# Attention and gated MLP for one token: output rows 16 partitions apart for one store, a split last weight piece, and merged folds

## The chip, the cores and the metric

The kernel runs on one core of one Trainium2 chip. The metric is the device time of one execution in microseconds. "Faster" or "slower" needs 2%. There is one trace, of one execution, for each kernel.

## The reference

For four sequences of one token each, an attention block over the last 4096 cache positions and a gated MLP are mixed by a sigmoid gate:

```python
def reference(A_x, A_k_cache, A_v_cache, A_wq, A_wo, B_x, B_W_gate, B_W_up, B_W_down, gate_w):
    x = A_x                                               # [4, 1, 512]
    g = _sigmoid((x * gate_w).sum(-1, keepdims=True))
    a = _A_ref(x, A_k_cache, A_v_cache, A_wq, A_wo)       # 32 heads, 8 kv heads, window 4096, Dh 128
    b = _B_ref(x, B_W_gate, B_W_up, B_W_down)             # relu(gate) * up, then down; F = 1792
    return g * a + (1 - g) * b                            # [4, 1, 512] bf16
```

What matters for time: 81 MB are read once (sixteen 4 MB loads of K and V, the rest weights), and only 4 KB are written.

## The kernel before

SyncE issues all loads in order through four slots of 4 MB. The last load is `wo`, the 4 MB of output weights, cut into six pieces so that the matmuls of one piece run while the next lands. Eight sets (4 sequences x 2 groups of 4 kv heads) go through scores, softmax and `PV`. `OQ` ("fold") picks each head's own block out of the `PV` result and lays it out for the output matmul. `EOQ` scales it by 1/rowsum and by the gate into `oq`. `WO` accumulates in one PSUM bank on top of the MLP (`FFN`), the left half of the columns in rows 0 to 3, the right half in rows 64 to 67.

```python
WO_PIECES = ((0, 8), (8, 16), (16, 24), (24, 28), (28, 30), (30, 32))   # of 32 head rows per partition
OUTT = 2
OW = 512 // OUTT
OR = 128 // OUTT
# order of work at the end:  ... PV(6), PT(7), RS(1), GU, PV(7), FFN, OQ(1), WO(0..5)
# OQ(0), the fold of sets 0 to 3, runs in the middle of the kernel

def store(E, e, t):
    E.op(lambda: e.dma_start(out.rearrange("b o d -> (b o) d")[:, OW * t:OW * t + OW], osum[OR * t:OR * t + 4, :]),
         ev=("OUT", t), waits=[("OSUM",)], ctr=f"d_out{t}")          # t = 0 on SyncE, t = 1 on ScalarE

def OQ(g):                                        # 16 matmuls of 128 columns
    ...
        mm(banks[tr(key)][r:r + 64, 0:128], R["fold"][:, 2 * cc + t, c, :], osb[:, :, x:x + 32], ...)

def WO(p):                                        # two matmuls a head row: left and right half
    lo, hi = WO_PIECES[p]
    w = [("WO", p)] + [("E", "OQ", g) for g in range(2)]
    for i in range(lo, hi):
        for j in range(OUTT):
            mm(banks[ACC][OR * j:OR * j + 4, 0:OW], oq[:, i, :], Wo[:, i, OW * j:OW * j + OW], False, i == 31, ...)

def EOQ(g):                                       # VectorE; oq is [128, 32, 4]
    E.op(lambda: v.tensor_tensor(oq[r, :, :].rearrange("p i b -> p b i"), ...))

def FIN():                                        # VectorE: PSUM to SBUF, 128 x 256
    E.op(lambda: v.tensor_copy(osum[:, :], banks[ACC][:, 0:OW]), ev=("OSUM",), waits=[("WOP", len(WO_PIECES) - 1)])
```

(`...` marks cuts.)

Of the kernel before, what the change touches and what calls it, by code (L numbers as in the profile page):

```python
# [11 lines left out]
B = 4  # L12
# [9 lines left out]
NTR = 2  # L22
NSC = 3
BIG = 1.0e30
WO_PIECES = ((0, 8), (8, 16), (16, 24), (24, 28), (28, 30), (30, 32))
OUTT = 2
OW = 512 // OUTT
OR = 128 // OUTT

class _Plan:  # L30

# [70 lines left out]
def _alloc(nc, ctx):  # L102
    R = {}

    def sb(name, shape, dt):
        R[name] = ctx.enter_context(nc.sbuf_tensor(name, shape, dt))

    sb("slots", [128, NSLOT, 16384], BF16)
    sb("kt", [128, 4, 4096], BF16)
    sb("sc", [128, 2048], BF16)  # L110
    sb("pe", [128, 2048], BF16)
    sb("pT", [128, 2, 2048], BF16)
    sb("qblk", [128, NSET, 2, 144, 2], BF16)
    sb("xsb", [4, 512], BF16)
    sb("xT", [128, 16], BF16)
    sb("gwT", [128, 4], BF16)
    sb("osb", [128, 4, 512], BF16)
    sb("oq", [128, 32, 4], BF16)
    sb("identb", [128, 128], BF16)
    sb("identf", [128, 128], FP32)  # L120
    sb("ones", [128, 128], FP32)
    sb("ee", [16, 128], FP32)
    sb("e4", [16, 128], FP32)
    sb("rfold", [128, 128], FP32)
    sb("grpb", [128, 128], BF16)
    sb("own8", [128, 8], FP32)
    sb("scl", [128, 8], FP32)
    sb("maskl", [128, 128], BF16)
    sb("maskr", [128, 512], BF16)
    sb("maskf", [128, 512], BF16)  # L130
    sb("gwB", [128, 4, 128], BF16)
    sb("fold", [128, 4, 4, 64], BF16)
    sb("mx4", [128, 4], FP32)
    sb("rd32", [128, 8, 4], BF16)
    sb("negmax", [128, 2], FP32)
    sb("rowsum", [128, NSET], FP32)
    sb("recip", [128, 2, 4], FP32)
    sb("ge", [128, 2, 4], FP32)
    sb("gp", [128, 2, 4], FP32)
    sb("gg", [128, 2, 4], FP32)  # L140
    sb("hg", [128, 14, 4], BF16)
    sb("osum", [128, OW], BF16)
    R["psum"] = ctx.enter_context(nc.psum_tensor("bank", [128, 8, 512], FP32))
    return R


def _order():
    o = [("CONST", k) for k in ("mask", "grp", "rfold")] + [("XT",), ("Z",), ("Q",), ("QT",), ("KT", 0, 0), ("KT", 0, 1), ("SC", 0, 0)]
    o += [("KT", 0, 2), ("SC", 0, 1), ("KT", 0, 3), ("SC", 0, 2)]
    for s in range(1, NSET):  # L150
        o += [("KT", s, 0), ("SC", s - 1, 3)] + [("RS", 0), ("OQ", 0)] * (s == 5) + [("SW", s - 1)]
        o += [("KT", s, 1), ("PT", s - 1), ("SC", s, 0), ("KT", s, 2), ("SC", s, 1), ("KT", s, 3)]
        o += [("SC", s, 2)] + [("PV", s - 1)] * (s < NSET - 1)
    s = NSET - 1
    o += [("SC", s, 3), ("SW", s), ("PV", s - 1), ("PT", s), ("RS", 1), ("GU",), ("PV", s), ("FFN",), ("OQ", 1)]
    return o + [("WO", p) for p in range(len(WO_PIECES))]


# [28 lines left out]
def _program(nc, plan, R, aps):  # L187
# [17 lines left out]
    Wq = slot("wq").rearrange("p (t f) -> p t f", t=4)  # L205
    Wg, Wu = slot("wg")[:, 0:4 * FF], slot("wg")[:, 4 * FF:8 * FF]
    Wd = slot("wd")[:, 0:14 * 512]
    Wo = slot("wo", 0).rearrange("p (i c) -> p i c", i=32)
    grelu, hrow, hT = sc[:, 0:448], sc[:, 512:960], sc[:, 1024:1472]

    trf, scf = {}, {}
# [26 lines left out]
    def sc_free(key):  # L238
        n = scf[key] - NSC
        return [("E",) + sck[n]] if n >= 0 else [("INIT",)]  # L240

    def set_of(s):
        return s % 4, s // 4

    def ob(s):
        return banks[OB[s % 2]]

    def store(E, e, t):
        E.op(lambda: e.dma_start(out.rearrange("b o d -> (b o) d")[:, OW * t:OW * t + OW], osum[OR * t:OR * t + 4, :]),
             ev=("OUT", t), waits=[("OSUM",)], ctr=f"d_out{t}")  # L250

    def sync(e):
        E = _Eng(plan, e, "sp")
# [4 lines left out]
        for it in _dma_order():  # L258
# [4 lines left out]
            elif k == "gw":  # L263
                load(("GW",), "d_gw", gwT[:, :], gate_w.rearrange("(p t) -> p t", t=4))
            elif k == "wq":
                load(("WQ",), "d_wq", slot("wq"), A_wq.rearrange("(p t) f -> p (t f)", t=4), waits=w)
            elif k == "wg":
                load(("WG",), "d_wg", Wg, B_W_gate.rearrange("(p t) f -> p (t f)", t=4), waits=w)
            elif k == "wu":
                load(("WU",), "d_wu", Wu, B_W_up.rearrange("(p t) f -> p (t f)", t=4), waits=w)  # L270
            elif k == "wd":
                load(("WD",), "d_wd", Wd, B_W_down.rearrange("(p i) c -> p (i c)", i=14),
                     waits=w)
            elif k == "wo":
                lo, hi = WO_PIECES[it[1]]
                load(("WO", it[1]), f"d_wo{it[1]}", Wo[:, lo:hi, :], A_wo.rearrange("(p i) c -> p i c", i=32)[:, lo:hi, :],
                     waits=w)
            else:
                b, qq = set_of(it[1])
                src = (A_k_cache if k == "k" else A_v_cache)[b, 4 * qq:4 * qq + 4, SK - WIN:SK, :]  # L280
                load((k.upper(), it[1]), f"d_{k}{it[1] % 3}", slot(*it), src.rearrange("h (r c) d -> r h (c d)", r=32),
                     waits=w)
        for t in range(0, OUTT, 2):
            store(E, e, t)
        E.wait([("OUT", t) for t in range(OUTT)])

    def gpsimd(e):
        E = _Eng(plan, e, "pool")
# [19 lines left out]
        op(lambda: e.memset(R["scl"][:, :], -SCALE), ("SCL",))  # L308
        aff(R["own8"][:, :], R["scl"][:, :], [[-16, 8]], 0, ge_, 0.0, ("OWN", 0))
        aff(R["own8"][:, :], R["own8"][:, :], [[16, 8]], 15, ge_, 0.0, ("OWN", 1), mult=-1)  # L310
        op(lambda: e.memset(R["fold"][:, :, :, :], 0.0), ("FOLD0",))
        for g in range(8):
            v = R["fold"][:, g % 4, :, :]
# [2 lines left out]
    def tensor(t):  # L316
# [75 lines left out]
                    mm(ob(s)[r:r + 64, :], pT[:, s % 2, x:x + 64], vv[:, f, :, c:c + 2, :], (f, c) in ((0, 0), (0, 2)),  # L392
                       (f, c) in ((3, 12), (3, 14)), ev=("PV", s) if (f, c) == (3, 14) else None, waits=w, pos=(0, r))

        def OQ(g):
            key = ("OQ", g)
            r = 64 * g
            for t in range(2):
                for cc in range(2):
                    for c in range(4):  # L400
                        x = 256 * t + 128 * cc + 32 * c
                        first, lastmm = (t, cc, c) == (0, 0, 0), (t, cc, c) == (1, 1, 3)
                        mm(banks[tr(key)][r:r + 64, 0:128], R["fold"][:, 2 * cc + t, c, :], osb[:, :, x:x + 32], first,
                           lastmm, ev=key if lastmm else None, pos=(0, r),
                           waits=tr_free(key) + [("NORM", 4 * g + 3), ("FOLD", 7)] if first else ())

        def GU():
            for n, (W, key) in enumerate(((Wg, "WG"), (Wu, "WU"))):
# [8 lines left out]
        def FFN():  # L417
            for i in range(14):
                for j in range(OUTT):
                    x = 512 * i + OW * j  # L420
                    mm(banks[ACC][OR * j:OR * j + 4, 0:OW], R["hg"][:, i, :], Wd[:, x:x + OW], i == 0, False,
                       ev=("FFN",) if (i, j) == (13, OUTT - 1) else None, waits=[("E", "HT"), ("WD",), ("G",)],
                       pos=(0, OR * j))

        def WO(p):
            lo, hi = WO_PIECES[p]
            w = [("WO", p)] + [("E", "OQ", g) for g in range(2)]
            for i in range(lo, hi):
                for j in range(OUTT):
                    mm(banks[ACC][OR * j:OR * j + 4, 0:OW], oq[:, i, :], Wo[:, i, OW * j:OW * j + OW], False, i == 31,  # L430
                       ev=("WOP", p) if (i, j) == (hi - 1, OUTT - 1) else None, waits=w if (i, j) == (lo, 0) else (),
                       pos=(0, OR * j))

        fns = dict(CONST=CONST, XT=XT, Z=Z, Q=Q, QT=QT, SC=SC, PV=PV, SW=SW, RS=RS, OQ=OQ, WO=WO, GU=GU, FFN=FFN)
        for it in order:
# [4 lines left out]
    for it in order:  # L440
# [27 lines left out]
        elif k == "PV":  # L468
            act.append(("NORM", it[1]))
        elif k == "OQ":  # L470
            dve.append(("EOQ", it[1]))
    dve.append(("FIN",))

    def qd(n):
# [8 lines left out]
    def vector(v):  # L483
# [61 lines left out]

        def ERS(g):
            key = ("RS", g)
            E.op(lambda: v.reciprocal(recip[:, 0, :], banks[tr(key)][:, 0:4]), ev=("E",) + key, waits=[key])
            E.op(lambda: v.tensor_tensor(recip[:, 1, :], recip[:, 0, :], gg[:, 0, :], ALU.mult), ev=("RG", g),
                 waits=[("E",) + key, ("G",)])  # L550

        def EOQ(g):
            key = ("OQ", g)
            r = slice(64 * g, 64 * g + 64)
            E.op(lambda: v.tensor_tensor(oq[r, :, :].rearrange("p i b -> p b i"),  # L555
                                         banks[tr(key)][r, 0:128].rearrange("p (b i) -> p b i", b=4),
                                         bc(recip[r, 1, :].unsqueeze(2), 2, 32), ALU.mult), ev=("E",) + key,
                 waits=[key, ("RG", g)])

        def H():  # L560
            def by_i(t):
# [6 lines left out]

        def EHT():
            E.op(lambda: v.transpose(hT, hrow), ev=("HT",), waits=[("H",)])  # L570
            E.op(lambda: v.tensor_tensor(R["hg"][:, :, :], hT.rearrange("p (i b) -> p i b", b=32)[:, :, 0:4],
                                         bc(gg[:, 1, :].unsqueeze(1), 1, 14), ALU.mult), ev=("E", "HT"),
                 waits=[("HT",), ("G",)])

        def FIN():
            E.op(lambda: v.tensor_copy(osum[:, :], banks[ACC][:, 0:OW]), ev=("OSUM",), waits=[("WOP", len(WO_PIECES) - 1)])  # L576
# [6 lines left out]
    def scalar(a):  # L583
# [15 lines left out]
                 waits=[("GW",)])  # L599

        def NORM(s):
            E.op(lambda: a.activation(osb[:, s % 4, :], ob(s), ACTF.Copy), ev=("NORM", s),  # L602
                 waits=[("PV", s)] + ([("OQ", 0)] if s >= 4 else []))

        def GE():
            for u in range(2):
# [13 lines left out]
        fns = dict(ECONST=ECONST, GWB=GWB, EQ=EQ, GE=GE, RELU=RELU, EXP=EXP, NORM=NORM)  # L620
        for it in act:
            fns[it[0]](*it[1:])
        for t in range(1, OUTT, 2):
            store(E, a, t)

    return [("tensor", tensor), ("vector", vector), ("scalar", scalar), ("gpsimd", gpsimd), ("sync", sync)]

# [27 lines left out]
```

## Time and profile before

| | before |
|---|---|
| median of the first 3 executions | 197.54 us (197.31 to 197.7) |
| span of the profiled execution | 195.6 us |
| DMA engines | 9 tenths busy or more in 38 of 40 slices |
| TensorE, VectorE busy | 62%, 63% |
| last `wo` landing, start of the last PSUM copy, start of the store issue | 192.84, 193.31, 193.77 us |

The page's rows for DMA; each digit is the busy share of one fortieth of the span in tenths, and below it the rate in GB/s:

```profile
DMA  6999999999999999999999999999999999999991
GB/s 221 442 423 436 429 442 436 419 436 429 436 456 429 437 426 436 429 429 429 436 429 436 426 429 429 429 429 429 429 426 429 429 405 434 448 429 403 417 402 53
```

The core reads at one steady rate, 402 to 456 GB/s in 38 of the 40 slices, until about 191 us. Work of the other engines is free as long as it does not delay a load or the last results. So the end of the kernel decides. The end of its chain of waits (start us, length us, what):

```profile
173.31 0.04 issue
173.35 19.49 DMA slots<-in_A_wo_dram
192.84 0.04 issue
192.89 0.40 PE bank L320 x4
193.29 0.02 issue
193.31 0.42 DVE osum L576
```

Read from the bottom: the copy waited for four matmuls, and those for a DMA that landed at 192.84. The timeline of the same stretch (start us, length us, engine, line, operation, count, idle time before it and who ended that):

```profile
187.00 1.91 PE L320 MATMUL bank<-slots,oq 128*4 128x256 bf16 x32 [0.63 <-DVE oq L555]
...
190.38 1.04 PE L320 MATMUL bank<-slots,oq 128*4 128x256 bf16 x16 [1.47 <-DMA slots<-in_A_wo_dram]
...
192.89 0.38 PE L320 MATMUL bank<-slots,oq 128*4 128x256 bf16 x4 [0.24 <-DMA slots<-in_A_wo_dram]
193.31 0.42 DVE L576 CAST osum<-bank 128x256 bf16<-128x256 f32 x1 [6.46 <-PE bank L320]
193.77 0.29 SPq L249 DMA_DIRECT2D out_dram<-osum  x1
193.77 0.62 ACTq L249 DMA_DIRECT2D out_dram<-osum  x1
```

TensorE idles before pieces of `wo`, ended by DMA: it keeps up. Every `wo` DMA over 128 rows raises its semaphore in 16 steps. The trace has the time of each. (A piece has landed when its last step has come: the last piece at 192.84, and its matmuls start at 192.89. The page counts 16 DMA engines. I read each step as the end of one engine's share; the trace names no engine.) For the last piece before (256 KB):

```
190.98 191.03 191.07 191.15 191.24 191.25 191.27 191.45 191.46 191.55 | 192.42 192.60 192.68 192.72 192.74 192.84
```

Ten steps come over a microsecond before the last one, and six come late. The change goes for that gap.

### The profile page before, as it was taken

The page shows a single profiled execution, that of the slowest core. Times are in us where ns is not written, and L with a number is a line of the kernel's source. Part 1 is how long each engine was busy: PE and PEld are TensorE (multiplying, and loading weights), DVE is VectorE, ACT ScalarE, POOL GpSimd, SP SyncE. Part 2 cuts the span into 40 slices and gives each one's busy share as a digit, 9 for nine tenths or more (in the row PEclk, how much of TensorE's full clock was granted, in tenths as well). Part 3 has the DMA queues.
Part 4 walks back from the last instruction along what each step waited for, and adds up shares of the span by engine and source line. Part 5 has one row for each costly group of instructions (what it writes and reads, how often), then busy time and mean ns, then how long its engine had stood idle before and what let it go on. Part 6 is the DMA issues. An engine that isn't in the chain of part 4 may idle for free.

```text
span 195.6 us, 1780 instructions
## 1 busy us (share of the span) xinstructions
PE 121.2 (62%) x741; PEld 50.9 (26%) x741; DVE 124.0 (63%) x153; ACT 27.3 (14%) x33; POOL 9.5 (5%) x25
## 2 busy tenths in 40 slices
PE   0418279465933894595468953893395557734954
PEld 0213123122411331142113521241141112412631
DVE  6104769999299819971998199819972997460000
ACT  2213000040130013001300131014001400420100
POOL 7830000000000000000000000000000000000000
PEclk9999957999999697999886999699999789997999
DMA  6999999999999999999999999999999999999991
GB/s 221 442 423 436 429 442 436 419 436 429 436 456 429 437 426 436 429 429 429 436 429 436 426 429 429 429 429 429 429 426 429 429 405 434 448 429 403 417 402 53
DMA packets 3919, 81.12 MB, mean 415 GB/s; under 512 B 572, under 2 KB 584, under 8 KB 968
## 3 DMA queue, kind: packets, MB, share of 16 engines
q1 hardware_dynamic: 3904, 81.01, 97.1%
q8 instruction: 6, 0.10, 0.2%
q14 instruction: 1, 0.01, 0.0%
q10 hardware_dynamic: 8, 0.00, 0.0%
HBM read 81.01 MB, written 0.00 MB: 414 GB/s over the span
## 4 chain that ended last, share of the span: by engine, by line
DMA 54%; DVE 30%; PE 9%; issue 5%; SPq 1%; ACT 0%
DMA slots<-in_A_k_cache_dram 38%; DVE kt L492 21%; DMA slots<-in_A_wo_dram 10%; PE bank L320 7%; DMA gwT<-in_gate_w_dram 6%; DVE sc L528 5%; DVE qblk L518 1%; SPq L256 1%; DVE pT L543 1%; PE bank L324 1%; DVE rd L532 1%; ACT gwB L598 0%; DVE negmax L538 0%; DVE oq L555 0%; DVE osum L576 0%
## 5 line engine op out<-in xcount | busy, mean ns | idle before, releaser
L492 DVE STREAM_TRANSPOSE kt<-slots 128x2048 f32<-128x2048 f32 x32 | 73.7, 2304 | 27.5 <-DMA slots<-in_A_k_cache_dram 27.5
L320 PE MATMUL bank<-kt,qblk 128*128 128x512 bf16 x256 | 71.4, 430 | 29.2 <-DVE kt L492 29.1
L320 PEld LDWEIGHTS bank<-kt,qblk 128*128 128x128 bf16 x256 | 24.9, 106 | 70.7 <-DVE kt L492 37.6
L320 PE MATMUL bank<-slots,pT 128*64 128x512 bf16 x256 | 32.0, 407 | 5.7 <-DMA slots<-in_A_v_cache_dram 5.7
L617 ACT ACTIVATE pe<-sc,negmax 128x2048 bf16<-128x2048 bf16 x8 | 16.0, 2002 | 60.3 <-DVE negmax L538 60.3
L528 DVE CUSTOM_DVE_ANT_0 sc<-bank,maskf 128x512 bf16<-128x512 f32 x32 | 21.1, 658 | 4.1 <-PE bank L320 4.1
L320 PEld LDWEIGHTS bank<-slots,pT 128*64 128x64 bf16 x256 | 15.0, 117 | 23.1 <-issue 13.1
L543 DVE STREAM_TRANSPOSE pT<-pe 128x2048 bf16<-128x2048 bf16 x8 | 18.5, 2312 | 2.2 <-ACT pe L617 2.2
L602 ACT ACTIVATE osb<-bank 128x512 bf16<-128x512 f32 x8 | 4.8, 597 | 81.5 <-PE bank L320 81.5
L320 PE MATMUL bank<-rd,grpb 128*128 128x32 bf16 x8 | 1.5, 192 | 21.0 <-DVE rd L532 19.3
L555 DVE TENSOR_TENSOR oq<-bank,recip 64x128 bf16<-64x128 f32 x2 | 0.9, 442 | 11.5 <-PE bank L320 11.4
L320 PEld LDWEIGHTS bank<-rd,grpb 128*128 128x128 bf16 x8 | 0.8, 97 | 24.7 <-DVE rd L532 22.7
L320 PE MATMUL bank<-slots,oq 128*4 128x256 bf16 x64 | 4.3, 272 | 2.6 <-DMA slots<-in_A_wo_dram 1.9
L496 DVE COPY xT<-bank 128x16 bf16<-128x16 bf16 x1 | 0.2, 167 | 8.2 <-PE bank L324 8.2
L320 PE MATMUL bank<-slots,xT 128*4 128x512 bf16 (+1 forms) x64 | 5.2, 483 | 0.0
L576 DVE CAST osum<-bank 128x256 bf16<-128x256 f32 x1 | 0.4, 425 | 6.5 <-PE bank L320 6.5
L518 DVE TENSOR_SCALAR qblk<-bank 32x64 uint32<-32x64 uint32 x16 | 2.9, 215 | 2.3 <-PE bank L324 2.2
L320 PE MATMUL bank<-maskr,maskl 128*128 128x512 bf16 x1 | 0.6, 609 | 5.9 <-POOL maskr L296 5.9
L324 PE MATMUL bank<-identb,xsb 4*128 4x4 bf16 x4 | 0.3, 166 | 5.4 <-DMA xsb<-in_A_x_dram 5.4
L320 PEld LDWEIGHTS bank<-slots,oq 128*4 128x4 bf16 x64 | 2.3, 83 | 4.4 <-DMA slots<-in_A_wo_dram 3.1
L296 POOL TENSOR_SCALAR_AFFINE_SELECT fold<-fold 128x256 bf16<-128x256 bf16 x8 | 3.3, 417 | 1.1
L487 DVE MEMSET qblk<- 128x2304 uint32 x1 | 2.0, 1978 | 1.4 <-PEq L640 1.4
(58 smaller groups left out, 42.2 us busy)
## 6 DMA issues: line engine op xcount, KB each, us to landing
slots<-in_A_k_cache_dram SPq DMA_DIRECT2D x8, 4096.0 KB, 25.2
slots<-in_A_v_cache_dram SPq DMA_DIRECT2D x8, 4096.0 KB, 30.6
slots<-in_A_wq_dram SPq DMA_DIRECT2D x1, 4096.0 KB, 12.4
slots<-in_A_wo_dram SPq DMA_DIRECT2D x3, 1024.0 KB, 16.4
slots<-in_B_W_gate_dram SPq DMA_DIRECT2D x1, 1792.0 KB, 19.7
slots<-in_B_W_up_dram SPq DMA_DIRECT2D x1, 1792.0 KB, 23.6
slots<-in_B_W_down_dram SPq DMA_DIRECT2D x1, 1792.0 KB, 18.6
slots<-in_A_wo_dram SPq DMA_DIRECT2D x1, 512.0 KB, 19.2
```

What stands on the lines that cost most here:

```text
L256: E.op(lambda: e.dma_start(dst, src), ev=ev, waits=waits, ctr=ctr)
L296: op(lambda: e.affine_select(dst, src, pattern, cmp, fill, base=base, channel_multiplier=mult), ev)
L320: E.op(lambda: t.matmul(out_, lhsT, rhs, start=start, stop=stop, tile_position=pos, skip_group_check=True), ev=ev, waits=waits)
L324: E.op(lambda: t.transpose(out_, in_, idn), ev=ev, waits=waits)
L487: E.op(lambda: v.memset(qblk[:, :, :, :, :].rearrange("p s h c e -> p (s h c e)"), 0.0), ev=("QZ",))
L492: E.op(lambda: v.transpose(kt[:, f, :].bitcast(FP32), slot("k", s)[:, 4096 * f:4096 * f + 4096].bitcast(FP32)), ev=("E", "KT", s, f), waits=w)
L518: E.op(lambda dst=dst, r=r, g=g: v.tensor_scalar(dst, src[r, g, 0:B, :, :], 0, None, op0=ALU.bitwise_or), ev=("E",) + keys[1] if (q, g) == ...
L528: E.op(lambda: v.tensor_tensor_reduce(sc[:, 512 * f:512 * f + 512], banks[scb(key)], R["maskf"][:, :], 1.0, -3.0e38, ALU.add, ALU.max, mx4 ...
L532: E.op(lambda: v.tensor_tensor(rd32[:, :, :], bc(R["own8"][:, :].unsqueeze(2), 2, 4), bc(mx4[:, :].unsqueeze(1), 1, 8), ALU.mult), ev=("MA ...
L543: E.op(lambda: v.transpose(pT[:, s % 2, :], pe[:, :]), ev=("E", "PT", s), waits=[("EXP", s)] + ([("PV", s - 2)] if s >= 2 else []))
L602: E.op(lambda: a.activation(osb[:, s % 4, :], ob(s), ACTF.Copy), ev=("NORM", s), waits=[("PV", s)] + ([("OQ", 0)] if s >= 4 else []))
L617: E.op(lambda: a.activation(pe[:, :], sc[:, :], ACTF.Exp, bias=negmax[:, s % 2:s % 2 + 1], scale=SCALE, accum_out=rowsum[:, s:s + 1]), ev= ...
```

## The change

Its intent has three parts, which I call S, P and F below.

- S: `oq` and `hg` get columns 16 apart (50 columns, the rest zero), so that the eight output rows come out at partitions 0, 16, ... 112, and one SyncE store takes all of them.
- P: `wo` is cut by half rows. The last piece is 64 KB, loaded as rows of 123, 3 and 2. It is meant to lie on three engines only, so that the others have 4 KB less to move.
- F: the folds of all eight sets are done once, at the end, with 16 matmuls of 256 columns instead of twice 16 of 128. Two small constants become bf16 too (their matmuls end before 8 us, and TensorE then waits until 13 us for the x load).

```diff
-WO_PIECES = ((0, 8), (8, 16), (16, 24), (24, 28), (28, 30), (30, 32))
+ST = OR // B
+LW = 3 * ST + 2
+WO_PIECES = ((0, 16), (16, 32), (32, 48), (48, 56), (56, 60), (60, 63), (63, 64))
+LOW3 = (0, 123, 126, 128)
...
-    sb("oq", [128, 32, 4], BF16)
+    sb("oq", [128, 32, LW], BF16)
...
-        o += [("KT", s, 0), ("SC", s - 1, 3)] + [("RS", 0), ("OQ", 0)] * (s == 5) + [("SW", s - 1)]
+        o += [("KT", s, 0), ("SC", s - 1, 3)] + [("RS", 0)] * (s == 5) + [("SW", s - 1)]
...
+                wo = A_wo.rearrange("(p i) c -> p (i c)", i=32)
+                for n, r in enumerate(wo_rows(it[1])):       # LOW3 slices for the last piece, else all 128
+                    load(("WO", it[1], n), f"d_wo{it[1]}", Wo[r, OW * lo:OW * hi], wo[r, OW * lo:OW * hi], waits=w)
...
-        for t in range(0, OUTT, 2):
-            store(E, e, t)
-        E.wait([("OUT", t) for t in range(OUTT)])
+        load(("OUT",), "d_out", out.rearrange("b o (t c) -> t (b o) c", t=OUTT),
+             osum[0:128:ST, :], waits=[("OSUM",)])
+        E.wait([("OUT",)])
...
-                        mm(banks[tr(key)][r:r + 64, 0:128], R["fold"][:, 2 * cc + t, c, :], osb[:, :, x:x + 32], first,
+                        mm(banks[tr(key)][0:64, 0:256], R["fold"][:, 2 * cc + t, c, :], osb[:, :, x:x + 32], first, lastmm,
...
+            for g in range(2):
+                r = slice(64 * g, 64 * g + 64)
+                E.op(lambda g=g, r=r: v.tensor_tensor(
+                    oq[r, :, 0:LW:ST].rearrange("p i b -> p b i"),
...
-        for t in range(1, OUTT, 2):
-            store(E, a, t)
```

More of the change, by code (lines that the diff above doesn't have):

```diff
@@ L116, in _alloc @@
     sb("gwT", [128, 4], BF16)
-    sb("osb", [128, 4, 512], BF16)
-    sb("oq", [128, 32, 4], BF16)
+    sb("osb", [128, NSET, 512], BF16)
+    sb("oq", [128, 32, LW], BF16)
     sb("identb", [128, 128], BF16)
@@ L121, in _alloc @@
     sb("ones", [128, 128], FP32)
-    sb("ee", [16, 128], FP32)
-    sb("e4", [16, 128], FP32)
+    sb("ee", [16, 128], BF16)
+    sb("e4", [16, 128], BF16)
     sb("rfold", [128, 128], FP32)
@@ L136, in _alloc @@
     sb("rowsum", [128, NSET], FP32)
-    sb("recip", [128, 2, 4], FP32)
+    sb("recip", [128, 4, 4], FP32)
     sb("ge", [128, 2, 4], FP32)
@@ L140, in _alloc @@
     sb("gg", [128, 2, 4], FP32)
-    sb("hg", [128, 14, 4], BF16)
+    sb("hg", [128, 14, LW], BF16)
     sb("osum", [128, OW], BF16)
@@ L154, in _order @@
     s = NSET - 1
-    o += [("SC", s, 3), ("SW", s), ("PV", s - 1), ("PT", s), ("RS", 1), ("GU",), ("PV", s), ("FFN",), ("OQ", 1)]
+    o += [("SC", s, 3), ("SW", s), ("PV", s - 1), ("PT", s), ("RS", 1), ("GU",), ("PV", s), ("FFN",), ("OQ",)]
     return o + [("WO", p) for p in range(len(WO_PIECES))]
@@ L207, in _program @@
     Wd = slot("wd")[:, 0:14 * 512]
-    Wo = slot("wo", 0).rearrange("p (i c) -> p i c", i=32)
+    Wo = slot("wo", 0)
     grelu, hrow, hT = sc[:, 0:448], sc[:, 512:960], sc[:, 1024:1472]
@@ L240, in sc_free, with wo_rows @@
         return [("E",) + sck[n]] if n >= 0 else [("INIT",)]
+    def wo_rows(p):
+        return [slice(a, b) for a, b in zip(LOW3, LOW3[1:])] if p == len(WO_PIECES) - 1 else [slice(0, 128)]
     def set_of(s):
@@ L246, in ob @@
         return banks[OB[s % 2]]
-    def store(E, e, t):
-        E.op(lambda: e.dma_start(out.rearrange("b o d -> (b o) d")[:, OW * t:OW * t + OW], osum[OR * t:OR * t + 4, :]),
-             ev=("OUT", t), waits=[("OSUM",)], ctr=f"d_out{t}")
     def sync(e):
@@ L275, in sync @@
                 lo, hi = WO_PIECES[it[1]]
-                load(("WO", it[1]), f"d_wo{it[1]}", Wo[:, lo:hi, :], A_wo.rearrange("(p i) c -> p i c", i=32)[:, lo:hi, :],
-                     waits=w)
+                wo = A_wo.rearrange("(p i) c -> p (i c)", i=32)
+                for n, r in enumerate(wo_rows(it[1])):
+                    load(("WO", it[1], n), f"d_wo{it[1]}", Wo[r, OW * lo:OW * hi], wo[r, OW * lo:OW * hi], waits=w)
             else:
@@ L310, in gpsimd @@
         aff(R["own8"][:, :], R["own8"][:, :], [[16, 8]], 15, ge_, 0.0, ("OWN", 1), mult=-1)
+        op(lambda: e.memset(R["hg"][:, :, :], 0.0), ("HG0",))
+        op(lambda: e.memset(oq[:, :, :], 0.0), ("OQ0",))
         op(lambda: e.memset(R["fold"][:, :, :, :], 0.0), ("FOLD0",))
@@ L393, in PV, with OQ @@
                        (f, c) in ((3, 12), (3, 14)), ev=("PV", s) if (f, c) == (3, 14) else None, waits=w, pos=(0, r))
-        def OQ(g):
-            key = ("OQ", g)
-            r = 64 * g
+        def OQ():
+            key = ("OQ",)
             for t in range(2):
@@ L402, in OQ @@
                         first, lastmm = (t, cc, c) == (0, 0, 0), (t, cc, c) == (1, 1, 3)
-                        mm(banks[tr(key)][r:r + 64, 0:128], R["fold"][:, 2 * cc + t, c, :], osb[:, :, x:x + 32], first,
-                           lastmm, ev=key if lastmm else None, pos=(0, r),
-                           waits=tr_free(key) + [("NORM", 4 * g + 3), ("FOLD", 7)] if first else ())
+                        mm(banks[tr(key)][0:64, 0:256], R["fold"][:, 2 * cc + t, c, :], osb[:, :, x:x + 32], first, lastmm,
+                           ev=key if lastmm else None, pos=(0, 0),
+                           waits=tr_free(key) + [("NORM", NSET - 1), ("FOLD", 7)] if first else ())
         def GU():
@@ L420, in FFN @@
                     x = 512 * i + OW * j
-                    mm(banks[ACC][OR * j:OR * j + 4, 0:OW], R["hg"][:, i, :], Wd[:, x:x + OW], i == 0, False,
+                    mm(banks[ACC][OR * j:OR * j + LW, 0:OW], R["hg"][:, i, :], Wd[:, x:x + OW], i == 0, False,
                        ev=("FFN",) if (i, j) == (13, OUTT - 1) else None, waits=[("E", "HT"), ("WD",), ("G",)],
@@ L426, in WO @@
             lo, hi = WO_PIECES[p]
-            w = [("WO", p)] + [("E", "OQ", g) for g in range(2)]
-            for i in range(lo, hi):
-                for j in range(OUTT):
-                    mm(banks[ACC][OR * j:OR * j + 4, 0:OW], oq[:, i, :], Wo[:, i, OW * j:OW * j + OW], False, i == 31,
-                       ev=("WOP", p) if (i, j) == (hi - 1, OUTT - 1) else None, waits=w if (i, j) == (lo, 0) else (),
-                       pos=(0, OR * j))
+            w = [("WO", p, n) for n in range(len(wo_rows(p)))] + [("E", "OQ")]
+            for x in range(lo, hi):
+                i, j = x // OUTT, x % OUTT
+                mm(banks[ACC][OR * j:OR * j + LW, 0:OW], oq[:, i, :], Wo[:, OW * x:OW * x + OW], False, i == 31,
+                   ev=("WOP", p) if x == hi - 1 else None, waits=w if x == lo else (), pos=(0, OR * j))
         fns = dict(CONST=CONST, XT=XT, Z=Z, Q=Q, QT=QT, SC=SC, PV=PV, SW=SW, RS=RS, OQ=OQ, WO=WO, GU=GU, FFN=FFN)
@@ L470, in _program @@
         elif k == "OQ":
-            dve.append(("EOQ", it[1]))
+            dve.append(("EOQ",))
     dve.append(("FIN",))
@@ L547, in ERS, with EOQ @@
             key = ("RS", g)
-            E.op(lambda: v.reciprocal(recip[:, 0, :], banks[tr(key)][:, 0:4]), ev=("E",) + key, waits=[key])
-            E.op(lambda: v.tensor_tensor(recip[:, 1, :], recip[:, 0, :], gg[:, 0, :], ALU.mult), ev=("RG", g),
+            E.op(lambda: v.reciprocal(recip[:, 2 * g, :], banks[tr(key)][:, 0:4]), ev=("E",) + key, waits=[key])
+            E.op(lambda: v.tensor_tensor(recip[:, 2 * g + 1, :], recip[:, 2 * g, :], gg[:, 0, :], ALU.mult), ev=("RG", g),
                  waits=[("E",) + key, ("G",)])
-        def EOQ(g):
-            key = ("OQ", g)
-            r = slice(64 * g, 64 * g + 64)
-            E.op(lambda: v.tensor_tensor(oq[r, :, :].rearrange("p i b -> p b i"),
-                                         banks[tr(key)][r, 0:128].rearrange("p (b i) -> p b i", b=4),
-                                         bc(recip[r, 1, :].unsqueeze(2), 2, 32), ALU.mult), ev=("E",) + key,
-                 waits=[key, ("RG", g)])
+        def EOQ():
+            key = ("OQ",)
+            for g in range(2):
+                r = slice(64 * g, 64 * g + 64)
+                E.op(lambda g=g, r=r: v.tensor_tensor(
+                    oq[r, :, 0:LW:ST].rearrange("p i b -> p b i"),
+                    banks[tr(key)][0:64, 128 * g:128 * g + 128].rearrange("p (b i) -> p b i", b=4),
+                    bc(recip[0:64, 2 * g + 1, :].unsqueeze(2), 2, 32), ALU.mult), ev=("E",) + key if g else None,
+                    waits=[key, ("RG", 1), ("OQ0",)])
         def H():
@@ L570, in EHT @@
             E.op(lambda: v.transpose(hT, hrow), ev=("HT",), waits=[("H",)])
-            E.op(lambda: v.tensor_tensor(R["hg"][:, :, :], hT.rearrange("p (i b) -> p i b", b=32)[:, :, 0:4],
+            E.op(lambda: v.tensor_tensor(R["hg"][:, :, 0:LW:ST], hT.rearrange("p (i b) -> p i b", b=32)[:, :, 0:4],
                                          bc(gg[:, 1, :].unsqueeze(1), 1, 14), ALU.mult), ev=("E", "HT"),
-                 waits=[("HT",), ("G",)])
+                 waits=[("HT",), ("G",), ("HG0",)])
         def FIN():
@@ L601, in NORM @@
         def NORM(s):
-            E.op(lambda: a.activation(osb[:, s % 4, :], ob(s), ACTF.Copy), ev=("NORM", s),
-                 waits=[("PV", s)] + ([("OQ", 0)] if s >= 4 else []))
+            E.op(lambda: a.activation(osb[:, s, :], ob(s), ACTF.Copy), ev=("NORM", s),
+                 waits=[("PV", s)])
         def GE():
```

## The prediction

> What bounds the kernel. The page puts the 16 DMA engines at 9 tenths busy or more in 38 of 40 slices at 403 to 456 GB/s, moving 81.1 MB; VectorE is at 63%, TensorE at 62%. In the chain of waits the whole stretch from 173.35 to 192.84 us is the landing of the output weights (wo). The kernel is DMA-bound to 192.84 us, and then a short serial tail runs, read from the timeline and the chain: 4 matmuls 0.40, PSUM copy 0.42, store issue from 193.77, last store landing 195.13, closing barrier, span end 195.6.
>
> 1. The last piece. The 16 semaphore steps of each DMA (the landings in the trace) do not come together. For the last 256 KB piece eleven engines land at 190.98 to 191.55 and five at 192.42 to 192.84. I read the late five as those that carried a 16 KB instruction fetch: the packet records show such packets of 0.92 to 1.06 us at 39, 72, 111, 146 and 183 us, and only three steps lag at 111 us. [...] The change moves the last 64 KB off the 16 engines: [...] So three engines get 42 or 43 rows of 512 B and thirteen get 4 KB less. Packets took 84 ns for 2048 B, 46 for 1024 and 26 to 32 for 512, so an estimate for 43 rows is 43 x 25 = 1.1 us; the three early engines would end at about 191.4 to 192.0, still before the late ones, which gain the 4 KB, about 0.17 us. I could not identify engines in the trace; if one of the first three is a late one, the last landing comes about 0.9 us later instead.
>
> 2. The last piece ends in 1 matmul, not 4 (0.40 to about 0.27 us): 0.1 us saved.
>
> 3. One store instead of two. In the trace the ScalarE store took 0.62 us to issue against SyncE's 0.29 and landed at 195.13 against 194.94: 0.15 to 0.2 us saved, all on the chain.
>
> 4. Merged folds. The late fold grows from 16 x 128 to 16 x 256 columns (1.08 to about 1.7 us), and two VectorE scalings of 0.45 follow instead of one. The wo matmuls then start at about 188 instead of 187.0; 32 of them take 1.91 us, so they have caught up by 190, before the third piece lands at 190.34. Off the chain. The larger memsets on GpSimd fall before 15 us, off the chain.
>
> Sum: -0.17 - 0.1 - 0.17 = about -0.45 us, 197.1. I shift slightly for the chance of about 25% that the three engines include late ones (then about +0.6). Neither case leaves the 2% band.
>
> Right if: steps of the last piece land by about 192.6 us or earlier, with the three engines not last; one matmul between the last landing and the copy; one store landing about 1.2 us after the copy; third wo piece still awaited by TensorE. Wrong if: the 512 B rows cost well above 25 ns each or fall on an engine delayed by an instruction fetch, the merged fold delays the matmuls past 190.3, or the store on fewer engines lands later.

The sum came to -0.17 - 0.1 - 0.17, about -0.45 us. That three engines take the last piece, and that these are early ones, stand in it as assumptions. The 0.17 us for 4 KB are two packets of 2048 B at the measured 84 ns, the 0.9 us for a late engine is the gap of 0.87 us between the tenth and the eleventh step above (191.55 to 192.42), and the chance of 25% is a guess.

## The result

| | before | after |
|---|---|---|
| median us (executions) | 197.47 (197.31 to 197.91, 6) | 197.59 (197.49 to 197.81, 6) |
| ratio of the fast runs, 95% interval | | 1.0004 (0.9992 to 1.0017) |
| span of the profiled execution | 195.6 | 196.1 |
| `wo` matmuls start, end | 187.00, 193.27 | 189.78, 193.46 |
| last `wo` landing, copy starts, store issue starts | 192.84, 193.31, 193.77 | 192.87, 193.51, 193.96 |
| store: first packet, last landing after the issue started | 0.76, 1.36 | 1.26, 1.71 |

A ratio is the mean time of one kernel's fast runs over the mean of the other's in the same rounds, so it is not quite the ratio of the quoted medians. The time is the same. The forecast gain of about 0.45 us (to 197.1) is not there. The profiled execution is 0.5 us longer than that of before, but it was one of the slowest two of its six, and that of before the fastest of its six.

The end of the chain of waits of the kernel after:

```profile
147.76 30.94 DMA slots<-in_A_v_cache_dram
178.70 0.14 issue
178.83 9.30 PE bank L326 x76
188.13 0.02 issue
188.16 0.73 DVE oq L560
188.89 0.01 issue
188.90 0.75 DVE oq L560
189.65 0.14 issue
189.78 3.70 PE bank L326 x64
193.49 0.02 issue
193.51 0.42 DVE osum L582
```

The steps of the last two pieces in this trace, first the piece `(60, 63)` over all 128 rows, then the eight steps of the split piece (its other three steps, at 174.45, 185.21 and 186.60, come with the issues of its three loads):

```
190.76 190.84 190.89 190.90 190.91 190.93 190.94 191.11 191.17 191.27 | 192.13 192.44 192.46 192.56 192.59 192.87
191.83 192.01 192.19 192.21 192.25 192.39 192.43 192.62
```

The `wo` load has left the chain. The last 15 us now go from the landing of the last V through TensorE (PV, FFN, fold), two scalings of `oq` and all 64 `wo` matmuls without a wait. The timeline of the same stretch:

```profile
188.16 1.48 DVE L560 TENSOR_TENSOR oq<-bank,recip 64x128 bf16<-64x128 f32 x2 [12.90 <-PE bank L326]
189.75 3.43 PEld L326 LDWEIGHTS bank<-slots,oq 128*50 128x50 bf16 x64 [1.91 <-issue]
189.78 3.68 PE L326 MATMUL bank<-slots,oq 128*50 128x256 bf16 x64 [1.67 <-DVE oq L560]
193.51 0.42 DVE L582 CAST osum<-bank 128x256 bf16<-128x256 f32 x1 [3.87 <-PE bank L326]
193.96 0.63 SPq L259 DMA_DIRECT2D out_dram<-osum  x1
```

Two differences stand out: there is no idle time ended by `wo` any more, and the one store takes 0.63 us to issue where SyncE's took 0.29.

Part of the late start seems not to come from the change. Stretches of the PV of the last set, kernel before first and kernel after second (stretch, then busy times by engine, the granted TensorE clock, DMA share, GB/s):

```profile
178.70:181.00 2.30, 2.28 (x12) 1.22 (x14) 0.00 (x0) 0.00 (x0) 0.00 (x0) 0.50 0.97 409
181.00:183.00 2.00, 2.00 (x20) 1.10 (x17) 0.00 (x0) 0.00 (x0) 0.00 (x0) 0.87 1.04 429
```

```profile
178.70:181.00 2.30, 2.17 (x12) 1.10 (x14) 0.00 (x0) 0.00 (x0) 0.00 (x0) 0.50 0.98 414
181.00:183.00 2.00, 2.00 (x12) 0.97 (x10) 0.00 (x0) 0.00 (x0) 0.00 (x0) 0.50 1.03 425
```

TensorE had been idle for 5.7 us in both, and the clock is granted at 0.50 when it starts again. Before, full speed came back at 181.5 us; after, only at 183.7. The 32 matmuls took 5.02 and 6.03 us. Over the 14 profiles they took 4.95 to 6.52 us, with merged folds (4.95 the shortest) and with split ones (6.47 the longest but one) alike. These 14 numbers are from one execution of each kernel, and what decides when full speed comes back they do not show. The clock differs between executions of one kernel: the mean granted clock was 0.887 to 0.904 over the six executions of after, and 0.887 to 0.919 over eleven of before.

### The profile page after: what moved, and what is told of

Read it like the earlier page. It is cut to its first block, busy times and chain, and to the rows that moved or that the text cites. A ratio compares the mean times of both kernels' runs of the same rounds, so it can differ in the third digit from the quotient of the medians.

```text
span 196.1 us, 1749 instructions
## 1 busy us (share of the span) xinstructions
PE 123.0 (63%) x723; PEld 53.3 (27%) x723; DVE 124.9 (64%) x153; ACT 27.1 (14%) x33; POOL 11.6 (6%) x27
## 4 chain that ended last, share of the span: by engine, by line
DMA 47%; DVE 25%; PE 20%; issue 6%; SPq 0%; ACT 0%
DMA slots<-in_A_k_cache_dram 25%; PE bank L326 18%; DVE kt L496 18%; DMA slots<-in_A_v_cache_dram 16%; DMA gwT<-in_gate_w_dram 6%; DVE sc L532 4%; PE bank L330 2%; DVE qblk L522 1%; DVE oq L560 1%; DVE rd L536 0%; DVE negmax L542 0%; SPq L259 0%; ACT gwB L604 0%; DVE osum L582 0%; DVE mx L532 0%
## 5 line engine op out<-in xcount | busy, mean ns | idle before, releaser
L326 PE MATMUL bank<-kt,qblk 128*128 128x512 bf16 x256 | 73.7, 441 | 26.8 <-DVE kt L496 26.8
L326 PEld LDWEIGHTS bank<-kt,qblk 128*128 128x128 bf16 x256 | 25.7, 109 | 70.0 <-DVE kt L496 34.5
L326 PE MATMUL bank<-slots,pT 128*64 128x512 bf16 x256 | 32.6, 413 | 5.7 <-DMA slots<-in_A_v_cache_dram 5.7
L560 DVE TENSOR_TENSOR oq<-bank,recip 64x128 bf16<-64x128 f32 x2 | 1.5, 734 | 12.9 <-PE bank L326 12.9
L326 PE MATMUL bank<-slots,oq 128*50 128x256 bf16 x64 | 3.7, 273 | 1.7 <-DVE oq L560 1.7
L326 PEld LDWEIGHTS bank<-slots,oq 128*50 128x50 bf16 x64 | 3.4, 104 | 1.9 <-issue 1.9
```

The source lines that it names most:

```text
L326: E.op(lambda: t.matmul(out_, lhsT, rhs, start=start, stop=stop, tile_position=pos, skip_group_check=True), ev=ev, waits=waits)
L560: E.op(lambda g=g, r=r: v.tensor_tensor(oq[r, :, 0:LW:ST].rearrange("p i b -> p b i"), banks[tr(key)][0:64, 128 * g:128 * g + 128].rearran ...
```

## The experiments

Twelve kernels, each with 5 rounds against the kernel before on the same chip. Medians of one row may be compared with the median of before in that row.

| kernel | P | S | F | median us | before | ratio (95%) |
|---|---|---|---|---|---|---|
| p_only | x | | | 197.35 | 197.35 | 1.0003 (0.9990 to 1.0016) |
| s_only | | x | | 197.71 | 197.35 | 1.0021 (1.0009 to 1.0033) |
| f_only | | | x | 197.39 | 197.35 | 1.0003 (0.9991 to 1.0015) |
| no_f | x | x | | 197.74 | 197.38 | 1.0020 (1.0006 to 1.0033) |
| no_s | x | | x | 197.30 | 197.38 | 0.9997 (0.9984 to 1.0009) |
| no_p | | x | x | 197.74 | 197.50 | 1.0013 (0.9999 to 1.0026) |
| after | x | x | x | 197.59 | 197.47 | 1.0004 (0.9992 to 1.0017) |
| rows128 | in part | x | x | 197.63 | 197.50 | 1.0013 (1.0000 to 1.0026) |
| two_sp | x | two stores | x | 198.34 | 197.38 | 1.0048 (1.0035 to 1.0060) |
| store_adjacent (wrong result) | x | other rows | x | 197.81 | 197.38 | 1.0025 (1.0012 to 1.0037) |
| store_linear (wrong result) | x | other order | x | 197.72 | 197.35 | 1.0030 (1.0014 to 1.0045) |
| store_plain8 (wrong result) | x | plain | x | 197.24 | 197.50 | 0.9986 (0.9974 to 0.9999) |
| before_sp_sp | | both on SyncE | | 197.56 | 197.50 | 1.0004 (0.9991 to 1.0016) |

My theory was that the parts have effects of their own which cancel, chiefly a gain at the last landing against a loss in the store. The rivals were that the split gains nothing, and that everything is noise.

The second table has what the traces say of the tail. The first number is from the landing of the third `wo` piece (a point that no part touches) to the landing of the fourth, the second to the last landing of all, the third to the start of the last PSUM copy. The fourth is the start of the `wo` matmuls. The last two are from the start of the store issue to its first packet and to the last store landing. All in us.

| kernel | 3rd to 4th | to last | to copy | `wo` starts | first packet | store landed |
|---|---|---|---|---|---|---|
| before | 1.25 | 2.50 | 2.97 | 187.00 | 0.76 | 1.36 |
| s_only | 1.27 | 2.54 | 3.03 | 188.62 | 1.27 | 1.71 |
| f_only | 1.23 | 2.51 | 2.98 | 189.64 | 0.76 | 1.37 |
| before_sp_sp | 1.26 | 2.53 | 3.00 | 187.16 | 0.76 | 1.53 |
| no_p | 1.27 | 2.55 | 3.21 | 189.74 | 1.27 | 1.72 |
| rows128 | 1.27 | 2.58 | 2.95 | 188.69 | 1.27 | 1.70 |
| p_only | 1.36 | 2.67 | 3.03 | 187.00 | 0.74 | 1.35 |
| no_f | 1.34 | 2.48 | 2.99 | 187.31 | 1.27 | 1.72 |
| no_s | 1.33 | 2.47 | 2.95 | 189.25 | 0.74 | 1.35 |
| two_sp | 1.34 | 2.45 | 2.96 | 189.36 | 1.26 | 2.29 |
| store_adjacent | 1.33 | 2.46 | 2.97 | 188.56 | 1.39 | 1.82 |
| store_plain8 | 1.34 | 2.45 | 2.96 | 188.88 | 0.77 | 1.22 |
| after | 1.33 | 2.44 | 3.08 | 189.78 | 1.26 | 1.71 |

(store_linear's profiled execution was the slowest of its six, 198.71 us; only its store is used, below.)

### p_only: the split alone

```diff
-WO_PIECES = ((0, 8), (8, 16), (16, 24), (24, 28), (28, 30), (30, 32))
+WO_PIECES = ((0, 16), (16, 32), (32, 48), (48, 56), (56, 60), (60, 63), (63, 64))
+LOW3 = (0, 123, 126, 128)
```

(with the loads and the loop of `WO` as in the change, on the kernel before)

> The kernel before with the last 64 KB of output weights as rows of 123, 3 and 2, nothing else. Theory A (each part has its own effect on the tail and they cancel): the late engines get 4 KB less each, one matmul follows the last landing, so the time falls by 0.2 to 0.35 us (about 197.2), and the last piece's three engines are not the last to land. Rival B (the split gains nothing, because the last landing of after was 192.87 against 192.84): within 0.1 us of before. Rival C (the parts are all below noise): as B, in all three runs of single parts.

No gain in the time: 197.35 against 197.35. The expected 0.2 to 0.35 us fails. The interval, -0.2 to +0.3 us, does not exclude a gain of 0.1. In this trace the split piece itself landed last, at 192.80, 0.19 after the piece before it. A sixth 16 KB instruction fetch began at 191.23, while the three engines were still working through their 512-byte rows (these ended at 191.99, against 191.78 in the trace of after, where no sixth fetch occurs). That the fetch hit one of the three is possible but not shown: the trace does not name engines, and in no_s, without a sixth fetch, the split piece also landed last, by 0.02 us.

### s_only: the one store alone

```diff
+ST = OR // B
+LW = 3 * ST + 2
-        for t in range(0, OUTT, 2):
-            store(E, e, t)
+        load(("OUT",), "d_out", out.rearrange("b o (t c) -> t (b o) c", t=OUTT),
+             osum[0:128:ST, :], waits=[("OSUM",)])
```

(with 50 columns in `oq` and `hg`, their zeroing, and no ScalarE store, on the kernel before)

> The kernel before with rows 16 partitions apart and one store, nothing else. Theory A: the one store takes 0.63 us to issue and lands about 1.7 us after its issue began, where the two stores landed after 1.36; so slower by 0.3 to 0.4 us (about 197.8). The prediction said 0.17 us faster. Rival C: no difference. Also: the scaling of oq should take 0.73 instead of 0.44 us, off the chain here.

0.36 us slower by the medians, and the interval excludes zero. The store accounts for it: it lands 1.71 us after its issue starts, where the two stores of before need 1.36. The end of its timeline, to be set against the 0.29 and 0.62 of before:

```profile
193.42 0.42 DVE L576 CAST osum<-bank 128x256 bf16<-128x256 f32 x1 [4.95 <-PE bank L320]
193.88 0.63 SPq L254 DMA_DIRECT2D out_dram<-osum  x1
```

The scaling of `oq` also took 0.75 us instead of 0.44, off the chain here.

### f_only: the merged folds alone

```diff
-[("RS", 0), ("OQ", 0)] * (s == 5)
+[("RS", 0)] * (s == 5)
-("FFN",), ("OQ", 1)]
+("FFN",), ("OQ",)]
```

(with one fold of 256 columns and two scalings, rows adjacent, on the kernel before)

> The kernel before with the folds of all sets merged, nothing else. Theory A: the fold grows by 0.6 to 0.85 us and one scaling of 0.44 is added, so the matmuls of the output weights start about 1.2 us later (188.2 to 189.3, by the clock granted around 179 to 184 us); they are 64 at about 57 ns, end at 192 to 193, so in executions where the clock is late TensorE ends together with the last landing: 0 to 0.2 us slower. Rival C: no difference, and TensorE still waits for the third piece.

No difference in the time. The trace has the late start, 189.64, at a PV of 6.2 us, and TensorE then runs its 64 matmuls without a wait. It ended at 193.44, 0.43 us after a last landing at 193.01, which is what the four matmuls of before need too (192.84 to 193.27). So here TensorE and DMA finish in a dead heat. The prediction's step 4, that the matmuls have caught up by 190 and that the folds are off the chain, is wrong; the effect that it gave, none, is right for this kernel.

### store_linear, two_sp, store_adjacent, before_sp_sp, store_plain8: why is one store slow?

```diff
 # store_linear
-        load(("OUT",), "d_out", out.rearrange("b o (t c) -> t (b o) c", t=OUTT),
+        load(("OUT",), "d_out", out.rearrange("b o (t c) -> (b o t) c", t=OUTT),
 # two_sp: one DMA for each half
+        for t in range(OUTT):
+            load(("OUT", t), f"d_out{t}", out.rearrange("b o (t c) -> t (b o) c", t=OUTT)[t],
+                 osum[OR * t:OR * t + OR:ST, :], waits=[("OSUM",)])
 # store_adjacent
-             osum[0:128:ST, :], waits=[("OSUM",)])
+             osum[0:2 * B, :], waits=[("OSUM",)])
 # before_sp_sp, on the kernel before; the ScalarE store is taken out
-        for t in range(0, OUTT, 2):
+        for t in range(OUTT):
             store(E, e, t)
 # store_plain8: the changes of store_linear and store_adjacent together
```

> The kernel after with the one store writing the eight rows in the order of the partitions, so that its DRAM side is one plain dimension of 8 rows (wrong result on purpose: rows permuted). If the split DRAM pattern (2 x 4 rows[...]) is what makes the one store slow, its issue falls from 0.63 to about 0.3 us[...]: 0.3 to 0.4 us faster than after. If the one store is slow whatever its pattern, same as after (about 197.6).

> The kernel after with its eight spaced rows stored by two DMAs of four rows, both from SyncE. If the step of 16 partitions is what makes the issue slow, each takes about 0.6 us and the last lands later than in after (over 1.9 us after the first issue began). If the number of rows in one DMA is what counts (about 0.08 us a row), each takes about 0.3 us and the last lands about 1.4 to 1.5 us after the first issue began: 0.2 to 0.3 us faster than after.

> The kernel after with its one store reading eight adjacent partitions instead of eight that are 16 apart (wrong result on purpose). If the step is the cost, the issue falls from 0.63 to about 0.3 us and the time by 0.3 us or more; if the count of rows is, the issue stays at 0.6 to 0.7 us and the time at after's.

> The kernel before with both of its stores issued from SyncE; rows adjacent, one plain row pattern, as before. So far each store that was slow (first packet 1.2 to 1.4 us after its issue began) was in a program whose only issuer is SyncE and had either a step of 16 partitions or a DRAM pattern of 2 x 4 rows; the fast ones (0.74 to 0.76) had neither and a second store on ScalarE beside them. Theory D (the pattern decides): the first packet again after about 0.75 us, issues of 0.3 us each, the last landing about 1.5 us after the first issue began; time within 0.15 us of before. Rival E (without a ScalarE store SyncE's is slow): first packet after about 1.26 us, issues of 0.6 us, last landing over 2 us after; 0.6 to 0.9 us slower.

> The kernel after with its one store reading eight adjacent partitions into eight rows in order (both sides plain; wrong result on purpose). Theory D: first packet about 0.75 us after the issue began instead of 1.26, 0.4 to 0.5 us faster than after (about 197.1 to 197.2). Rival E: as after, about 197.6.

The first three guesses all fell. A plain DRAM side did not help, four rows instead of eight did not help (each of two_sp's issues took about 0.6 us, 0.62 and 0.56), and adjacent partitions did not help. The five together, with SyncE's stores of before and after, give one table:

| SyncE store | SBUF side | DRAM side | issue us | first packet | its landing |
|---|---|---|---|---|---|
| before | 4 adjacent rows | one row step | 0.29 | 0.76 | 1.17 |
| before_sp_sp, first | 4 adjacent rows | one row step | 0.29 | 0.76 | 1.18 |
| store_plain8 | 8 adjacent rows | one row step | 0.29 | 0.77 | 1.22 |
| after | 8 rows, 16 apart | 2 x 4 rows | 0.63 | 1.26 | 1.71 |
| two_sp, first | 4 rows, 16 apart | one row step | 0.62 | 1.26 | 1.69 |
| store_linear | 8 rows, 16 apart | one row step | 0.69 | 1.32 | 1.75 |
| store_adjacent | 8 adjacent rows | 2 x 4 rows | 0.75 | 1.39 | 1.82 |

Either irregularity alone, the partition step of 16 or a second row dimension in DRAM, costs 0.33 to 0.46 us of issue and 0.5 to 0.6 us to the first packet; both together (after) cost no more than one. The trace of before already held a sign of it: its K and V loads, whose DRAM side has two row dimensions (`r h`), took 0.53 to 0.64 us to issue, and the weight loads, with one, 0.33 to 0.44 (0.39 for `wq`, which is as large as a K load). The row count made no difference (0.29 us of issue with four plain rows and with eight), and neither did a second issuer: before_sp_sp stores from SyncE only and is as fast (0.29 us, first packet after 0.76), which settles the rival. What inside the issue takes the time is not visible. (ScalarE's plain store in before also took 0.62 us to issue, but its first packet came after 0.86 us; that was not tested further.) The issues of store_plain8, store_adjacent and store_linear, beside the 0.63 of after:

```profile
193.46 0.42 DVE L582 CAST osum<-bank 128x256 bf16<-128x256 f32 x1 [4.72 <-PE bank L326]
193.91 0.29 SPq L259 DMA_DIRECT2D out_dram<-osum  x1
```

```profile
193.79 0.75 SPq L259 DMA_DIRECT2D out_dram<-osum  x1
```

```profile
194.84 0.69 SPq L259 DMA_DIRECT2D out_dram<-osum  x1
```

store_plain8 is 0.26 us faster than before by the medians (0.9986). Its store lands 1.22 us after the issue starts, where the two of before need 1.36, so one store can be the better one if both sides are plain. (P and F are in this kernel too, and its interval barely excludes 1.) Its rows are the wrong ones, so it is no solution. two_sp pays the slow issue twice and was the slowest of all.

### no_s, no_f, no_p, rows128: one part taken out of the change

```diff
 # no_s: rows adjacent, two stores
-ST = OR // B
-LW = 3 * ST + 2
+ST = 1
+LW = B
 # no_f: OQ(0) in the middle of the kernel and OQ(1) at the end, as before
 # no_p
-WO_PIECES = (... (56, 60), (60, 63), (63, 64))
-LOW3 = (0, 123, 126, 128)
+WO_PIECES = (... (56, 60), (60, 64))
+LOW3 = (0, 128)
 # rows128: the last 64 KB stay a piece, over all rows at once
-LOW3 = (0, 123, 126, 128)
+LOW3 = (0, 128)
```

> The kernel after with the store undone: rows adjacent again (four columns of weights instead of 50) and two stores, on SyncE and ScalarE. Theory A: 0.35 us faster than after, about 197.2 to 197.3, since s_only cost 0.36; the store lands about 1.36 us after its issue begins, and each scaling of oq takes 0.44 us again. If the merged folds were what costs in after, it stays near 197.6.

no_s is 0.08 us below its before, where after was 0.12 above, and it lands its stores after 1.35 us: as expected, if smaller. The store is what after pays.

> The kernel after with the folds split again as in before (one fold at about 115 us). Theory A: TensorE starts the output weights about 1.3 us earlier than in after and waits for the last pieces again, so the one matmul after the last landing ends about 0.3 us after it and not 0.6; time at or 0.1 to 0.2 us below after (197.4 to 197.6), because the one store still costs 0.35. A sixth instruction fetch near 191.3 us comes back with the 16 extra matmuls, and can fall on one of the three engines, which takes the gain away again.

The time stays where the store puts it, 0.36 above before. The text expected it at after's or below, and after was 0.12 above its before, so that expectation fails. TensorE starts `wo` at 187.31, waits for pieces again, and the copy comes 2.99 us after the third piece instead of after's 3.08. The copy was expected 0.3 us after the last landing and came 0.51 after it (192.96 to 193.47), because the piece that lands last is not the split one. I come back to that below. A sixth 16 KB fetch did come, at 191.84; here the split piece landed at 192.83, before the other.

> The kernel after with the pieces of the kernel before (the last 128 KB and 128 KB as one DMA each over 128 rows). Last landing about 2.5 us after the third piece's; time 0 to 0.15 us above after, since TensorE is at most 0.1 us behind the landings there.

As expected in time (0.24 above its before, where after was 0.12 above). TensorE, late again (PV 6.2 us), is what the copy waits for: 3.21 us after the third piece.

> The kernel after with its last 64 KB over all 128 rows at once, on 16 engines. If confining them to three engines gains its 4 KB on the late engines and costs about 0.1 us in the fourth piece (1.33 to 1.37 us after the third, against 1.23 to 1.27 in the kernels without it), then here the fourth piece comes 1.25 us after the third again, the last two together take about 0.6 us more after the fifth, and the last landing comes about 2.5 us after the third piece's instead of 2.45. Time within 0.15 us of after. One matmul follows the last landing, so the copy starts about 0.35 us after it.

The fourth piece is back at 1.27, as expected, and the last landing comes at 2.58, a little later than the expected 2.5. The time is 0.13 above before, as after's 0.12. With one matmul behind it the copy starts 0.37 us after that landing. So the plain version of P, a small last piece over all 128 rows, reaches the copy as soon (2.95) as the three-engine version does at its best (2.95 to 2.99). Before's pieces, where TensorE is not behind, reach it at 2.97 to 3.03.

## Why the prediction was right and wrong

The text was right that the time stays in the 2% band. That is no support for its picture: the band is almost 4 us wide on either side, and none of the twelve kernels is more than 0.96 us from before. The number inside the band was not right: the text forecast about 0.45 us of gain, and there is none. Of the four signs that it set for being right, one came true (the split piece was in by 192.62, and its engines were not last). More than one matmul stood between the last landing and the copy, the store landed 1.7 us after the copy's end and not about 1.2, and TensorE no longer waited for the third piece. So the right class is luck as far as the mechanism goes: every effect at stake was small against the band. Point by point:

1. "The last piece", -0.17. The counts fit the picture, though the text miscounted: ten early steps and six late, not eleven and five. The number of late steps in the trace equals the number of instruction fetches so far (packets of 16 KB in the profile's instruction queue), one of 8 KB at 64 us included: three at 110 us, four at 139, five at 149, six from the first `wo` piece on, in before and after. In the `wo` pieces the first late step comes 0.85 to 0.93 us after the last early one. That they are the engines of the fetches is inferred from these counts. Three engines for the split piece fit the trace as well: it rises by eight single steps besides those of its issues, and its packets come in at most three streams. The three engines were early ones in the trace of after (all steps of the split piece in by 192.62, last landing 192.87), and their 512-byte packets came 23 to 25 ns apart, close to the estimate. What the sum missed: the fourth piece lands 1.33 to 1.36 us after the third in the seven tabled kernels with the three-engine rows and 1.23 to 1.27 in the six without, so about 0.08 us is given back first. rows128 differs from after in this only, so by these traces the cause is those rows; by what path they slow the others was not tested. From the fourth landing to the landing of `(60, 63)` it then takes about 1.11 us where the last piece of before took 1.26, so the 4 KB did save there, about 0.15 of the expected 0.17. Net: 2.44 to 2.48 instead of 2.50 to 2.55 to the last landing, about 0.06 us, with p_only (2.67) as an exception the other way. At the copy even that is gone: where TensorE is not behind it starts 2.95 to 3.03 us after the third piece with the three-engine rows and 2.97 to 3.03 with before's pieces. So for the split the first rival holds, and p_only's tie is what the traces show too.

2. "The last piece ends in 1 matmul, not 4", -0.1. This step contradicted the first. If the three engines finish early, the piece that lands last is the one before, `(60, 63)`, and its three matmuls and the last one follow it: four, as before. The copy starts 0.51 us after the last landing in no_f, two_sp, store_adjacent and store_plain8, against 0.47 in before. Only where the last piece lands well after the one before it is it 0.36 (p_only) or 0.37 (rows128); in no_s, where it lands 0.02 after, it is 0.48. So the split and the one-matmul tail exclude each other.

3. "One store instead of two", -0.17. This failed, with the sign, and s_only's interval excludes the rival that everything is noise. Measured: +0.35 from issue to landing in s_only, no_f, no_p and after, and +0.36 in the time of s_only. The text had compared the issue of a plain store with another plain one and had taken the new one to cost as little. Its patterns are not plain on either side.

4. "Merged folds", called off the chain. Mis-sized in each term of the profiled execution. Merged fold 1.91 us instead of 1.7; each scaling 0.73 instead of 0.45. PV took 1.0 us longer than in the trace of before, by the clock. So `wo` started at 189.78 instead of 188, and never had to wait. The copy came 0.64 us after the last landing instead of 0.51. That is about 0.13 us in an execution with a late clock, and nothing in one with an early one (store_adjacent and store_plain8: PV 4.95 and 5.06 us, `wo` from 188.56 and 188.88, copy after 0.51). The scaling is longer because S spaces its output: neighbouring elements are 100 bytes apart instead of 8, and kernels with adjacent rows take 0.43 to 0.45 us, the spaced ones 0.73 to 0.75. By what mechanism the spacing costs this is not shown.

Sum with the measured terms: -0.06 for the split, +0.04 for the matmuls behind the last landing (0.51 against 0.47), +0.35 for the store, 0 to +0.13 for the folds: +0.33 to +0.46 against before. The two profiled executions differ by 0.49 in span, but they are not typical ones. The median says +0.12, and the interval of the ratio (-0.16 to +0.34 us, from 0.9992 and 1.0017 times 197.47) only just reaches the lower end of that. Taking S out or putting it in, by the medians against before, is worth 0.20 to 0.36 us: 0.36 (s_only), 0.36 (no_f less p_only), 0.20 (no_p less f_only), 0.20 (after less no_s). Whether F or P really softens the store's cost, or those are differences of single medians, stays open; 0.1 us is below what five rounds resolve. That the store costs time is shown (s_only, and the stores of the same kernel with plain patterns); that it alone decides the time of after is not.

Where the expected gain went: more than half was never there (a plain store's cost was assumed, and a matmul tail that the split excludes), and most of the landing's gain was given back in the piece before. Of the correct kernels none is clearly faster than before. The lowest, no_s (197.30, 0.9997), is a tie. The runs point to one version more: folds and pieces as in before, and both halves copied into the same four partitions (by two engines at once), so that one plain store of four full rows takes them. By store_plain8's landing of 1.22 us against 1.36 an estimate is 0.14 us, if the two copies together take no longer than the one copy does now. It was not run.

## What to carry to other kernels

Before two DMAs are merged into one, compare the patterns and not the count: here a store that was plain on both sides issued in 0.29 us and landed in about 1.2, and one step of 16 partitions or one more row dimension made it land 0.5 to 0.6 us later, where a second plain store cost 0.2 to 0.35 (1.36 and 1.53 us for both, against 1.18 for the first). In a chain of landing, matmul, copy and store, ask of each saving which event comes last after it, and do not count a saving at the early branch and one at the late branch together. Work moved from an idle middle to the end is free only while the chain in front of it has slack in the slowest execution too, here with the TensorE clock released 2 us later in one trace than in the other.

## Further figures from the traces

- Counted from the start of the issue, the first packet of a SyncE store came after 0.74 to 0.77 us where both sides were plain, and after 1.26 to 1.39 us with a partition step of 16 or a 2 x 4 row pattern. The issue of the first store of SyncE took 0.27 to 0.29 us in the plain case and 0.62 to 0.75 us in the others.
- In the trace of after, with loads issued since 147.8 us still to land, SyncE's issue of the 3-row load took 10.7 us (174.3 to 185.0) and that of the 2-row load 1.3 us, where the other `wo` loads took 0.31 to 0.44. What held them is not shown. It cost nothing here because SyncE had nothing else to issue until 193.9; a store behind it would have waited.
- No idle time of TensorE is put down to an instruction fetch in the traces of before and after, but each 16 KB fetch was one DMA packet of 0.92 to 1.10 us in them, and in this kernel, which is bound by DMA, the count of late semaphore steps rises by one with each fetch, six of 16 at the end, 0.9 us behind the others.
- A 64 x 128 bf16 write of VectorE took 0.43 to 0.45 us with elements 8 bytes apart and 0.73 to 0.75 us at 100 bytes.
